# Keys and queries of four batches in two groups of six PSUM banks, in an attention and ELU feed-forward kernel with a planned order

## The chip, the cores and the metric

One core of a Trainium2 chip runs the whole kernel. Times are device microseconds of one execution, from three executions of the kernel before. The core has five engines with a queue each: PE (TensorE, the matmuls), ACT (ScalarE), DVE (VectorE), POOL (GpSimd) and SP (which here only issues transfers). Matmul results go to PSUM, which the code uses as eight banks of 128 x 512 fp32.

## What is computed

The reference is a linear attention with an exponential feature map, and a feed-forward layer with ELU behind it. All tensors are fp32; 8 batches, 8 heads, 576 rows, head size 64, 128 features.

```python
def phi(x):
    proj = np.einsum('bhsd,df->bhsf', x, w_phi)
    proj = proj - np.max(np.abs(proj), axis=-1, keepdims=True)
    return np.concatenate([np.exp(proj), np.exp(-proj)], axis=-1)
q_p, k_p = (phi(q), phi(k))
kv = np.einsum('bhsf,bhsd->bhfd', k_p, v)
z = np.sum(k_p, axis=2)
num = np.einsum('bhsf,bhfd->bhsd', q_p, kv)
den = np.einsum('bhsf,bhf->bhs', q_p, z)[..., None] + 1e-06
...
h = x @ w_in                                   # 4608x512 @ 512x2048
g = np.where(h > 0.0, h, np.exp(np.minimum(h, 0.0)) - 1.0)
out = g @ w_out                                # 4608x2048 @ 2048x512
```

## The kernel before

**Attention by quads.** Four heads of one batch are a quad; there are 16 (`plan_quad`, i = 0 to 15; batch b = i // 2). Of the 576 rows, 512 are the main part and 64 the tail. Keys and queries are transposed (`kT`, `qT`), by PE in the first quads and by SP's transposing transfers from quad 5 on (L555). Then come the projections by `w_phi`. Head size 64 fills only half of PE's rows, so two heads are projected side by side by matmuls of 64 rows (`project_halves`, L672, matmul at L680; `queries_f`, L839, matmul at L843). All other matmuls of the kernel's steady part use 128 rows. The planner calls the 64-row form `mode` 1, and adds 0.095 us to its own estimate for each change of mode.

Per quad the main part makes three kinds of PSUM results. Keys: four banks (`pk`, 16 matmuls), each read by a maximum on DVE (`m_k`, L701) and two exponentials on ACT (`EK`, L739). Queries with rows on the partitions: four banks (`pk`, 8 + 8 matmuls), read by a maximum on DVE only (`m_q`). Queries with features on the partitions: four banks (`pq`, 2 + 2 matmuls of 512 columns), read by two exponentials on ACT each (`Eq`, L906). In batches 2 to 7 they are issued in three groups of four banks: keys; first half of the queries in both forms; second half in both forms (`both`, L867). Tails have small groups of their own with 128 rows.

The rest of a quad: `vs` and `vst` on POOL (L790, L800), `pkv` on PE (L949) with a copy `kv`, `pn` and `pnt` on PE (L1003, L1031), combined by DVE into `tot` (L1052, L1058), divided by DVE and POOL into `x`, transposed into `xT`.

**Feed-forward by chunks.** `plan_chunk` takes 512 rows at a time: eight chunks of main rows, and a ninth made of all tails. A `ph` bank gets four matmuls of 512 columns (L1296, in the first chunk eight of 256, L1311). Then ACT makes `e_sb` (exp, L1324), POOL `u_sb` (minus one, L1328), DVE `gT` (L1340), which frees the bank. A `po` bank takes 16 matmuls over four blocks of 128 rows (L1398), in four ops of four; a copy to `o_sb` on ACT or DVE (L1424) frees it and SP stores it (L1433). The last block of the last chunk is cut into two pieces of 256 columns; their stores are shared between SP and ACT (L1437).

**The order.** Each step is an op with a cost for each engine that can run it, what it depends on, the banks that it takes anew (`new`) and those that it reads (`uses`). `Planner.run` walks through a model of time: for each free engine it takes the ready op with the lowest rank that `fits`. Ranks are a table of two digits per op (`RANKS`, L34). `fits` (L211) caps the banks: a kind `first` or `second` op waits until few enough are held, `ph` has at most four, `po` at most two. Where PE is idle in the model during its first 60 us, it writes filler matmuls (L263 to L268, `fill` L1601). So each engine's instruction order is fixed when the program is built, and at run time each engine follows it and waits for semaphores.

Of the kernel before, what the change touches and what calls it, by code (L numbers as in the profile page):

```python
# [8 lines left out]
FP32 = mybir.dt.float32  # L9
# [25 lines left out]
    "0Q0R0Y0U0l0kHn0+103Y0g0h121B0j14181G161D1I1M1k1F1O1f1L1o1q1r7Q6eBq7B07927YWx4eS7"  # L35
    "04ER1HDHPmPl0KDyDx0LDwD+0HEBDv0JE0E1DzD-251K1p231i1u1v4W5QEWSXEhEpBeEo5I5GS4S2TW"
    "PkPhPj5FS3TUTVPiU9Ud5bUc5SRr97SqU+98SsVQ9IV3V59KSwU-8pV2V4Ti202RUz2C2DVF2f0r8Y8m"
    "H3A8Aw0200064l4dS95JUnEnCQWaQGQHWZQ3OLWVQCP-WhQ5QDWiQ4QBQFQE1h2m261t2a1y2s5P5EUp"
    "UmTgTTTfTZ5O5TUsUrEzSaULUS5RUkUTE+UQUOEd0tGi3IR90x809G0s9g9y1dKwKL0PHuGY7nKKKx7s"
    "2t2u8w3n3VJy3o382q2JDn4KHP2K2G3H1a1m2y3l6k0O934u6M6O2Z9N4T617-2x9V3U8a4R398X2e63"  # L40
    "422p8j2i7A5Y5wEx6R9e3O4hEuAC3c1W01F03W3a2E0EHZ3X3g1T17F24X9F6515Eb485D6f0FBP4q4i"
    "Cx0i9x3R7pCjA3847y5i899bBH3mJ47Z7+223T8+8r3S6V8-418dAA7bDE8V1g7X8JA+BQ4L4f3uSb4+"
    "Pg0m7e3Z8K2v8oDiB7B8DhBSBGDgB3AvHvBRB4VTE-EfBJBI36293534283B33271e9Y9Z787790911l"
    "248O8P2+322-312HEt1V1Z1Y3M8M406J3NHNAq3eHKHt3dHwAr3fA4HQ5C9J9+Ee7P7O5fDo6AAh5HS8"
    "5KUo0n7t3E6N038l8W544z8k5M5N8z5L5cEv5Z5eDeB6BM1X1b3+0o1J0p0q0G0C2F3bEqEr5u5v5t5z"
    "2I1jElEm6u6t6r6q3jEaBXBW7W79D24rDm7a8q8U6wA78u6T8h8s6BAa8y6S8iF37f0W0X6C5aB-AeDI"
    "1c2n7oD1AQ2lIdBh0d2rKqBm7d3xIL4s6s4t9kIGA94MIsA6AF7TFs9lAB3QC39r2w8v3KQp7VEsFQ7q"
    "2MHUF-7lC+7rFp7m7h7UF67JC564CY7c2jBaAV6HC78tAT9s8f9v8nBd2hAUAi5-D71zFK75E2AdAbCM"
    "FH5o5p8FO46p87212B2O2A3P6Y372N3kAs2WCJ4JHO2L4pC69QBDBv9P9OBuBBBCBw9L9MF52Q2PA-B0"
    "9o8C858A8B191A2d8Z8b6P5x5y6K2c9D9E6i6g6h6j5VAM9u9t5s4n4c4m4jBnIVI+50JbIx59IeI-Bi"  # L50
    "JCJ01N6QDZ9h3h3i3r7x5d535+5l2g3JAo4C44An4D45Ap4E4IAm4746867R7S4A499T1C1E3y2o9d9R"
    "3LAfAcAOANARAP3zCRC43v3G3w3F4a4P4H4G3D4VJY9m5B7kFGFn7jF7G17iFZF+9zBO9w7MF8Fo8N7K"
    "7LGQFI8E6l7EG2FrGw7gGJ5rEyBZGPGhBTB5GvGTC11sD5GZAJMSHVETNU4g5kLAMFHBJlBj4oFh3qCI"
    "5AByQqAj3-CEUqAlBzGkP1CXBL96VSCUDRCdRwCZJHCaRvCsL7JURkCuDJIz6WOU9CRRR3RJ6IJi99Fu"
    "IOGf8LSpFT8T8g7GOSLfNG2X2S2U2T9X9aA26Z6-1n43C0BU130y9i0w0zBV0-0vBc0u11IH7u7v1+1-"
    "7262668D6774735WFvFx1R1Q1P1S5mHkHlGjGnGmGlAW9pADAEFN5X76ASGtG6GMGOG8GuHCGXFlGNGW"
    "HDGKEcFqGL5hEYEXDB8I1U2z6D7w5U8SAL514xAK5658AH4y4wAI4-52Cc3t3s574v888382817D8G6L"
    "5n4Y4b2V2Y4k305gDODN6d6c6b6a60Bg1w1x4ZGg4FDu8cCSVwRy9fSdSEAkQuVWCTUlVRCWVvRxRlHg"
    "HhA09A7NLF4UMo8RMd5jLO7FJn3pNHIaNj5qNpIbMuD0DkIDMwFeBpJTDdWeC9CvLjBEJzDUFyBFIXJK"
    "Jx8eSuIuK4HIFcHfHMDcRhJAMDMINEGqFwOpIUGrDCF9MGEwI8KpK3J1ItLQSeM8PRS6D4RWWJBNJEHq"  # L60
    "P0P3DDWgHGCoENWOWYWuLpB26n9n6mGeDr2b2kCKDG68CnOIGzH7ONG+IBOPH8H1OOGyIFJ2CrCtH0G-"
    "550A0D090B0f4Q6GPoPnKcLHKSKR6EOdOeLKLbLaLL9jIq3C3AMcJ3B16FMrEHBrBsClCNC8HxNqBbIh"
    "OgCADsBtBxJ-71700T0SFJFL4BEj69BKJhGHG5KNGCG7KMGFGGJjMBGEUiC26oGDGB4O0b0a4N0Z0c0e"
    "6XNRNQGUGaGVGb6UK7K6MZMVN5MYD6SBE4E5Mv6+NFJcDAHaSvI5GpTqRzRTO7J6RVNTMeRUOaMgRQOm"
    "OlJGJZFP9SWIQIDtAuJVTBKZAgEFHLPeBfKPMzPDDlI3PaOvLRLlQtP7I9CzLMORUgDWLIQVVaKmRSPG"
    "LrKyO9OzVyNSS0PNTaWqSMPLOcVxJdMsO+FAFDOrMiF4IIL5NrFbHTNDRNOwCwScPtDfG0EUESJ8IrEO"
    "L1M9KsU7K5MAMEM-NVGIMK080M8x0NIw0V9qA5FOFS9cCmIWJvJrJWK8K9EiK1K2EgJuJw8QDbDaKAMk"
    "LVKgKeKfKdKjKi9-MHMJLwL-LuLvAtOZOYLSLCLDLTCC7zLgLhLUHpP4HoP5DMIcHJD3QoSADFQJSFCp"
    "WlWsDKSGWvMxCyC-PbQS9BA19HPxAyBoH6KEW9H9WCKIGxKJKFH2KHKGJ5LzL+W8WWFdFiFjFgFkH-Fm"
    "CHQgQdCPCOAzAxCGWwSHTH9W9UTJCkWtTFTGBlQWNcCqRaLeIKHSL8HWFMPJSJL4PFThLGL6JSFEJkVO"  # L70
    "VPQ-IEEkU5OhKDN0LNOCFRMqE7PcFUNPECPpAXNME8QZISRID8P9ImRGDqJMSyRLWFJJS+RHTEJNSzVN"
    "S1InRgNiNfJ7IvKU8HI4RjKYOoEZTnOxNWJLKkNhLiWfL9KhDSI6W1NeKXLYK-I7MtMOMRN7MPUyJsLZ"
    "N2NAT9RdLPObNtTCT7RfOi7C95CL94KbQ9K005OnHHCDHmVlW6W4VjW3W7WRSQSRVnW5SUWUWBWXWGWH"
    "H+KnNJKoWMF1FBOJR4R6TuTrTvTmOQOEO8WnWkWoWpPELJVbUfTYGcP2GdQ7FfG4ICKrJ+KCDYBkHdEP"
    "GRIACeAGIYCBPZQYVzWAPBJDNnKQCfOGJePITcGSPHTbHrU2U3U8U0U6HRO1O0SPSOOjPrOBOAODO6O5"
    "CgI0I1LyM0LxM1CVLoLqPWPVPTPUJtLtQ2Q1M2LkE3NNFVREIgHARMTpQaMTITIiRFRDSxGsIfIlRiHj"
    "HzQnIpNOJBLBMWMNCiVGH5MXQAS5HyMMRKLcNZN9V7LdMhT8RPWSG3N3RcKvSWT6QOKtR+N4JXRmT0T2"
    "MyVmSVT3PYNCGAT5ReKOUhPzO3PMIoTAO-WEO2T1JIPqIyS-POTeNvPyTdTOUJJfQlTsSDUHSCRbP8Ty"
    "UCRpUDQ0VfSkSmUKVEM+NI4SBAWLB9VHWQJ9HFQUQRCFEQHYN+NyHeNmN-HcNsNwHbNuNzJaPwPvU4U1"
    "SgJPJFJOJQHsHiIjFYFXEDEEEAE9JoAYAZEKEMDQDPNLFWEJEIELMmQfMlQxL2M7M5LXLsHELWW0M4ML"  # L80
    "IQM3MjKlM6HXKuTNKaJRP6BYRtUVKWFaFzUbUaIP6x7HQM7I6zQN6v6yTwD9B+UYUXL0MbTRMaDjMpMn"
    "MQFCFFV6UvV8UwKVINIMOtK+OuKzNBQTQeQhRqN8UAN1UBT4SYUeN6TQSZOTNYSSOVSTTLStTKTDG9Tk"
    "TlQmOkTtPsShVgRoLnSLUNSiSIPCR0RnPPUtOHUIToJqNoSlLmQjMCSnROUWQXRsQvUuRYTzPuT-PKUG"
    "LEPQQKSjVoIJQ8T+WDL3QyTxNdTPOfRuVkVAQwUENgQbVZVCSrKTWrTMTjVDSoP+OFVIVKV1V+NbTSVq"
    "WcVdWmMURXQsPfQzR2PXPAUFVhJpTXVBQQWyKBVJRCOqR7V0IkNaUPVMUxOySNVLNXOKWjVcQiTIPSVX"
    "WKNkSKV-JgVYR5VrQrQkQcWdR8VVNlWNRBMfVuVpOXIRW2WbOWNxWTVtPdQ+VUVeWPRAR-CbFtGoH4NK"
    "URChDpE6EVOsR1DLDTDVDXOMV9UMUUViRZUZUjVsSf0IQPEGIZJmQ6QLI2"
# [37 lines left out]
class Planner:  # L125
# [43 lines left out]
    def run(self):  # L169
# [8 lines left out]
        mode = 0  # L178
        pending = []
        landed = []  # L180
        dma = 0.0
# [54 lines left out]
        while todo:  # L236
            started = False
            for e in ready:
                if free[e] > now:
                    continue  # L240
                best = None
                for at, o in ready[e]:
                    if at > now or o.engine or not fits(o, e):
                        continue

                    if any(
                        c < o.cost[e]
                        and free[x] <= now
                        and not any(a <= now and y is not o for a, y in ready[x])
                        for x, c in o.cost.items()  # L250
                    ):
                        continue
                    if best is None or o.rank < best.rank:
                        best = o
# [64 lines left out]
def kernel(  # L319
# [30 lines left out]

    DMA_QUAD = 5
# [161 lines left out]
    def plan_quad(i):  # L513
# [198 lines left out]
        for cs in ((0,), (1,), (2,)) if i == 0 else ((0, 1), (2,)):  # L712
            tail = cs == (2,)

            def keys(e, cs=cs):
                for c in cs:
                    project_halves(0, range(4 * c, 4 * c + 4), main_banks[c])

            o = add(
                {"PE": 0.11 if tail else 0.22 * len(cs)},  # L720
                (lambda e: project(0, 4, tail_bank))
                if tail
                else keys,
                [moved[0][-1] if tail else moved[0][cs[0]], *old("kv"), landed["w_phi"]],
                new=[tail_bank] if tail else [x for c in cs for x in main_banks[c]],
                mode=0 if tail else 1,
                key=first + 0.4 * tail if i != 1 else 0.35 + 0.01 * tail,
            )
            ops["k"].append(o)
            for c in cs:  # L730
                k_of[c] = o
# [96 lines left out]
        ops["q"], m_q, Eq_ops = [], [], {}  # L828
        m_qs = {0: [], 1: [], 2: []}
        for c in range(3):  # L830
# [3 lines left out]
            blocks = slice(c, 8, 2) if halves else slice(4 * c, 4 * c + 4)  # L834

# [29 lines left out]
            if c < 2 and b > 1:  # L865
# [15 lines left out]
            ops["q"] += [o] if o is o_f else [o, o_f]  # L881
# [12 lines left out]
            for par, bank in enumerate(pair_f):  # L894
# [12 lines left out]

                for sg in range(2):
                    Eq_ops[c].append(
                        add(  # L910
                            {"ACT": 0.48 if c < 2 else 0.27},
                            lambda e, sg=sg, f=exp_q: f(e, sg),
                            [o_f, landed["zero"]] if c == 2 else [o_f],
# [3 lines left out]
                    )  # L917

# [357 lines left out]
    def plan_chunk(ch):  # L1276
# [108 lines left out]
        if ch == B:  # L1385
            pieces[-1:] = [(3, 0, DM // 2), (3, DM // 2, DM)]
        for tt, o0, o1 in pieces:
# [3 lines left out]
            for part in range(n_parts):  # L1391
                jts = range(part * N_JT // n_parts, (part + 1) * N_JT // n_parts)

                def mm2(e, tt=tt, part=part, jts=jts, o0=o0, o1=o1, bank=bank):
# [22 lines left out]
                    key=2 * ch + 4.6 + 1.5 * (4 * tt + part) / N_JT + 0.1 * (o0 > 0),  # L1417
                )
                mm2s[ch].append(o)
            t = {}  # L1420

            def out_copy(e, o0=o0, o1=o1, bank=bank, t=t):
                t["o"] = moesm.tile([P, DM], FP32, name="o_sb", bufs=2)[:, o0:o1]
                (nc.scalar.copy if e == "ACT" else nc.vector.tensor_copy)(  # L1424
                    t["o"], bank.tile
                )

            def store(e, tt=tt, o0=o0, o1=o1, t=t):
# [6 lines left out]
                for j, eng in enumerate((nc.sync, nc.scalar)):  # L1435
# [3 lines left out]
                        in_=t["o"][j * TAIL:(j + 1) * TAIL, :],  # L1439
# [6 lines left out]
                [o, back(outs, 2)],  # L1446
# [194 lines left out]
```

## Time and profile before

| | us |
|---|---|
| median of three executions | 359.37 (359.02 to 361.77) |
| the profiled execution | 360.69 |
| its span, first to last instruction | 358.9 |

| engine | busy us | share of the span | instructions |
|---|---|---|---|
| PE | 349.1 | 97% | 3453 |
| DVE | 266.4 | 74% | 575 |
| ACT | 259.2 | 72% | 570 |
| POOL | 242.9 | 68% | 342 |

Busy PE counts a matmul from its start to the modelled end of its way through the array, so matmuls overlap in it; how fast PE works is read from start to start. Whoever an engine waited for is inferred from semaphores. The mean granted clock of PE is 0.995 of full speed.

### The profile page before, as it was taken

How to read it: one execution, taken by the hardware profiler on the slowest of the kernel's cores; microseconds unless marked ns; L12 is line 12 of the kernel's file. 1: busy time of each engine (PE TensorE's matmuls, PEld its weight loads, DVE VectorE, ACT ScalarE, POOL GpSimd, SP SyncE). 2: the span in 40 equal slices, each digit the busy share in tenths (PEclk: the TensorE clock that was granted, in tenths of full speed). 3: DMA queues.
4: the chain of work that ended last, by engine and by line, in shares of the span. 5: the costliest groups of instructions: out<-in, count | busy, mean ns of one | idle time of the engine just before them, and what ended most of it. 6: DMA issues, size and time to landing. Idle time of an engine off the chain costs nothing.

```text
span 358.9 us, 9072 instructions
## 1 busy us (share of the span) xinstructions
PE 349.1 (97%) x3453; PEld 205.5 (57%) x3453; DVE 266.4 (74%) x575; ACT 259.2 (72%) x570; POOL 242.9 (68%) x342
## 2 busy tenths in 40 slices
PE   7898999999999999999999999999999999999995
PEld 6676778656554655455555555555646454444444
DVE  6999699989996889679988989979876466024400
ACT  5997899897778886987889877996594555234411
POOL 9899869699769777867866694299674755034400
PEclk9998999999999999999999999999999999999999
DMA  8999999996886839979966752362130200110013
GB/s 171 232 242 205 211 187 238 142 170 170 147 109 127 123 79 206 173 116 191 151 99 155 154 83 64 92 186 45 35 92 32 62 3 29 58 61 29 29 60 88
DMA packets 84108, 43.46 MB, mean 121 GB/s; under 512 B 54624, under 2 KB 77536, under 8 KB 84064
## 3 DMA queue, kind: packets, MB, share of 16 engines
q1 hardware_dynamic: 57552, 26.59, 33.1%
q0 software_dynamic: 25760, 15.47, 31.1%
q10 hardware_dynamic: 752, 0.82, 0.8%
q8 instruction: 27, 0.44, 0.5%
q14 instruction: 17, 0.14, 0.1%
HBM read 36.77 MB, written 9.44 MB: 129 GB/s over the span
## 4 chain that ended last, share of the span: by engine, by line
PE 91%; ACT 7%; DMA 1%; issue 0%; POOL 0%; SPq 0%; ACTq 0%
PE po L1398 35%; PE ph L1296 31%; PE pkv L949 5%; PE pk L680 5%; PE ph L1311 4%; PE pn L1003 4%; ACT EK L739 3%; PE pq L843 2%; ACT Eq L906 2%; DMA v_b<-in_k_dram 1%; PE pnt L1031 1%; PE tr L619 1%; PE pk L662 1%; ACT EKt L739 1%; PE pq L855 0%; PE pn L1017 0%
## 5 line engine op out<-in xcount | busy, mean ns | idle before, releaser
L1398 PE MATMUL po<-w_out_sb,gT 128*128 128x512 bf16 (+1 forms) x592 | 136.2, 374 | 0.0
L1328 POOL TENSOR_SCALAR u_sb<-e_sb 128x512 bf16<-128x512 f32 x144 | 88.1, 618 | 60.8 <-ACT e_sb L1324 56.3
L1340 DVE SCALAR_TENSOR_TENSOR gT<-u_sb,ph 128x512 bf16<-128x512 bf16 x144 | 95.8, 680 | 40.2 <-POOL u_sb L1328 40.0
L1324 ACT ACTIVATE e_sb<-ph 128x512 f32<-128x512 f32 x144 | 86.5, 610 | 47.8 <-PE ph L1296 43.3
L1296 PE MATMUL ph<-xT,w_in 128*128 128x512 bf16 x448 | 108.4, 380 | 0.0
L1398 PEld LDWEIGHTS <-gT 128*128 128x128 bf16 x592 | 54.7, 98 | 57.9 <-issue 2.4
L906 ACT ACTIVATE Eq<-pq 128x512 bf16<-128x512 f32 x128 | 70.2, 643 | 12.1 <-PE pq L843 11.8
L1296 PEld LDWEIGHTS <-w_in 128*128 128x128 bf16 x512 | 53.6, 114 | 43.1 <-issue 2.1
L739 ACT ACTIVATE EK<-pk 128x512 bf16<-128x512 f32 x128 | 68.1, 641 | 4.3 <-PE pk L680 4.3
L790 POOL TENSOR_TENSOR vs<-v_b,em 128x512 bf16<-128x512 f32 x64 | 65.8, 1048 | 0.0
L701 DVE TENSOR_REDUCE m_q<-pk 128x4 f32<-128x512 f32 (+1 forms) x80 | 47.8, 629 | 11.4 <-PE pk L680 11.1
L701 DVE TENSOR_REDUCE m_k<-pk 128x4 f32<-128x512 f32 (+1 forms) x80 | 47.5, 629 | 7.0 <-PE pk L680 5.2
L1100 POOL TENSOR_TENSOR x<-tot,rec 128x576 bf16<-128x576 f32 x28 | 31.9, 1152 | 13.1 <-DVE rec L1096 13.1
L1424 ACT COPY o_sb<-po 128x512 f32<-128x512 f32 (+1 forms) x26 | 15.0, 577 | 24.8 <-PE po L1398 24.8
L1052 DVE TENSOR_TENSOR tot<-pn,w 128x260 f32<-128x260 f32 x64 | 26.8, 423 | 3.2 <-PE pn L1003 2.0
L1058 DVE TENSOR_TENSOR tot<-tot,pn 128x260 f32<-128x260 f32 x64 | 26.2, 418 | 0.4
L1003 PEld LDWEIGHTS <-Eq 128*128 128x128 bf16 x448 | 19.9, 97 | 8.3 <-issue 0.5
L1003 PE MATMUL pn<-kv,Eq 128*128 128x65 bf16 x448 | 22.4, 194 | 0.0
L949 PEld LDWEIGHTS <-EK 128*128 128x128 bf16 x512 | 18.8, 98 | 3.7 <-issue 0.3
L949 PE MATMUL pkv<-vs,EK 128*128 128x65 bf16 x512 | 20.7, 194 | 0.0
L800 POOL TENSOR_TENSOR vst<-v_tail,em 128x260 bf16<-128x260 f32 x32 | 19.6, 621 | 0.7 <-ACT em L768 0.6
L1311 PE MATMUL ph<-xT,w_in 128*128 128x256 bf16 x128 | 18.2, 280 | 0.0
(92 smaller groups left out, 319.1 us busy)
## 6 DMA issues: line engine op xcount, KB each, us to landing
out_dram<-o_sb SPq DMA_DIRECT2D x32, 256.0 KB, 2.4
v_b<-in_v_dram SPq DMA_DIRECT2D x6, 1024.0 KB, 6.0
k_b<-in_k_dram POOLq DMA_DIRECT2D x7, 512.0 KB, 8.9
q_b<-in_q_dram POOLq DMA_DIRECT2D x7, 512.0 KB, 10.1
w_in<-in_moe_w_in_dram POOLq DMA_DIRECT2D x2, 1024.0 KB, 19.1
w_out_sb<-in_moe_w_out_dram POOLq DMA_DIRECT2D x4, 512.0 KB, 22.0
v_b<-in_v_dram POOLq DMA_DIRECT2D x2, 512.0 KB, 10.0
v_b<-in_v_dram POOLq DMA_DIRECT2D x1, 1024.0 KB, 12.5
```

Of the source, the lines that this page charges most:

```text
L701: nc.vector.tensor_reduce(dst, src, axis=AX.X, op=ALU.max, apply_absolute_value=True)
L739: nc.scalar.activation(EK()[:, 2 * c + par, sg, :] if c < 2 else EKt[:, sg, :], bank.tile[:, 0:n, :].rearrange("p a b -> p (a b)"), ACT.Ex ...
L790: nc.gpsimd.tensor_tensor(st["vs"][:, sg, :, r, 0:D], kqv[b, 2][:, o:o + 2 * HW].rearrange("p (c n d) -> p c n d", c=2, d=D), by_head(st[" ...
L906: nc.scalar.activation(dst, src, ACT.Exp, scale=1.0 - 2.0 * sg)
L949: nc.tensor.matmul(pkv[:, c, sg, :], st["EK"][:, 2 * s + t % 2, sg, (2 * c + t // 2) * F:(2 * c + t // 2 + 1) * F,] if t < NT else EKt[:, ...
L1003: nc.tensor.matmul(pt[:, t, :], st["Eq"][:, par, s, sg, o:o + P], st["kv"][:, s, c, sg, :], start=True, stop=True,)
L1296: nc.tensor.matmul(ph, w_in_of(ct, jt), xTs[ch][:, ct, :] if ch < B else xT_tail[:, ct // 2, :, ct % 2, :], start=(ct == 0), stop=(ct == N ...
L1311: nc.tensor.matmul(bank.tile[:, j, :], w_in_of(ct, jt + j), xTs[ch][:, ct, hf * CHUNK // 2:(hf + 1) * CHUNK // 2], start=(j == 0 and ct == 0),
L1324: nc.scalar.activation(t["e"], flat(bank.tile), ACT.Exp)
L1328: nc.gpsimd.tensor_scalar(t["u"], t["e"], -1.0, 1.0, op0=ALU.add, op1=ALU.mult)
L1340: nc.vector.scalar_tensor_tensor(dst, u, 0.0, bank.tile, op0=ALU.min, op1=ALU.max)
L1398: nc.tensor.matmul(bank.tile, gTs[ch][:, jt, tt * P:(tt + 1) * P], w_out_sb[:, jt, o0:o1], start=(jt == 0), stop=(jt == N_JT - 1),)
```

## The change

There are three edits, and a new table of ranks.

In batches 4 to 7 (`b > MERGED`) the 64-row work of a quad is issued in two groups of six banks: the four key banks with the first two query banks (`q_first`), and the rest, that is the first half's `pq` pair, the second half's `pk` pair and `pq` pair. The exponentials of the first half then hang on the second group. The key group now also depends on the first part of `qT` and on the `pn` ops of the quad two before (`old("out")`).

In the planner, while an op that takes more than four banks is ready and doesn't fit, no op of a later rank that takes a bank may start on that engine.

In the last chunk, the last block is cut into 256, 128 and 128 columns, and the pieces share one `o_sb` tile.

The ranks are new for all ops (2109 before, 2103 after), so the order of every engine differs from the first microseconds on, also in batches 0 to 3. Filler matmuls become 132 where there were 117.

```diff
 RANKS = (
-    "0Q0R0Y0U0l0kHn0+103Y0g0h121B0j14181G161D1I1M1k1F1O1f1L1o1q1r7Q6eBq7B07927YWx4eS7"
+    "0t12141E1R1T8c1U1b6-1H1M1Q1Y1O1f1V1X1Z1k1m1q1u1g1v1r1i1x221tNx4iOS4-074Q7UBL0587"
...
                 best = None
+                first = min(
+                    [o.rank for at, o in ready[e]
+                     if at <= now and len(o.new) > 4 and not fits(o, e)],
+                    default=DONE,
+                )
                 for at, o in ready[e]:
                     if at > now or o.engine or not fits(o, e):
                         continue
+                    if o.new and o.rank > first:
+                        continue
...
-            def keys(e, cs=cs):
+            with_q = b > MERGED and not tail
+            if with_q:
+                q_first = [Bank("first") for _ in range(2)]
+
+            def keys(e, cs=cs, with_q=with_q):
                 for c in cs:
                     project_halves(0, range(4 * c, 4 * c + 4), main_banks[c])
+                if with_q:
+                    project_halves(1, range(4), q_first)
...
-                [moved[0][-1] if tail else moved[0][cs[0]], *old("kv"), landed["w_phi"]],
-                new=[tail_bank] if tail else [x for c in cs for x in main_banks[c]],
+                [moved[0][-1] if tail else moved[0][cs[0]], *old("kv"), landed["w_phi"]]
+                + ([moved[1][0], *old("out")] if with_q else []),
+                new=new + (q_first if with_q else []),
...
-            if c < 2 and b > 1:
+            if c < 2 and b > MERGED:
+                if c == 0:
+                    o, o_f = ops["k"][0], None
+                    ops["q"].append(o)
+                    rest = [(queries_f, pair_f)]
+                else:
+                    rest = [(queries, pair), *rest, (queries_f, pair_f)]
+
+                    def others(e, rest=rest):
+                        for f, _ in rest:
+                            f(e)
+
+                    o = o_f = add(
+                        {"PE": 0.66}, others, deps,
+                        new=[x for _, p in rest for x in p], mode=1, key=key,
+                    )
+            elif c < 2 and b > 1:
...
         if ch == B:
-            pieces[-1:] = [(3, 0, DM // 2), (3, DM // 2, DM)]
+            pieces[-1:] = [
+                (3, 0, DM // 2), (3, DM // 2, 3 * DM // 4), (3, 3 * DM // 4, DM)
+            ]
...
-                t["o"] = moesm.tile([P, DM], FP32, name="o_sb", bufs=2)[:, o0:o1]
+                if o0 == 0:
+                    t["o"] = moesm.tile([P, DM], FP32, name="o_sb", bufs=2)
                 (nc.scalar.copy if e == "ACT" else nc.vector.tensor_copy)(
-                    t["o"], bank.tile
+                    t["o"][:, o0:o1], bank.tile
                 )
```

## Prediction

> **What bounds the kernel now.** I read first, on the page, the shares of the chain of work that ended last and the slice rows of TensorE (PE) and of its clock.
>
> ```profile
> PE   7898999999999999999999999999999999999995
> ...
> PEclk9998999999999999999999999999999999999999
> ...
> PE 91%; ACT 7%; DMA 1%; issue 0%; POOL 0%; SPq 0%; ACTq 0%
> ```
>
> PE carries 91% of the chain. A slice is 9 us: only in the first four (to 36 us) and the last is PE less than full. The list of waits, asked for PE from 60 us to the end, is empty. So after 60 us time leaves only if PE gets less work, and comes only if PE starts to wait. Three stages matter.
>
> The opening, in windows of 2 us (us, then busy time of PE, weight loads, DVE, ACT, POOL, then clock, DMA share, GB/s):
>
> ```profile
> 28.00:30.00 2.00, 1.18 (x34) 1.01 (x30) 2.00 (x6) 2.00 (x5) 1.98 (x3) 1.00 1.30 191
> 30.00:32.00 2.00, 1.16 (x21) 0.80 (x17) 2.00 (x6) 2.00 (x8) 1.99 (x5) 1.00 1.35 205
> 32.00:34.00 2.00, 1.90 (x29) 1.91 (x30) 2.00 (x7) 0.86 (x2) 2.00 (x4) 0.62 1.13 213
> 34.00:36.00 2.00, 2.00 (x17) 1.68 (x15) 1.43 (x6) 1.01 (x1) 1.99 (x4) 0.52 1.16 209
> ```
>
> DVE, ACT and POOL are full while PE has gaps; then PE gets work, and runs it at half clock: in the chain, 16 transposes take 1.71 us there (107 ns each). From 5.7 to about 32 us the chain is mostly ACT (EK and Eq exponentials).
>
> The middle, from the timeline of PE (start, us, line, shape, count):
>
> ```profile
> 200.26 2.76 PE L1296 MATMUL ph<-xT,w_in 128*128 128x512 bf16 x12
> 202.95 0.40 PE L680 MATMUL pk<-w_phi_both,qT 64*128 64x128 bf16 x8
> 203.18 0.38 PE L843 MATMUL pq<-qT,w_phi_both 64*128 64x512 bf16 x2
> 203.49 1.04 PE L1398 MATMUL po<-w_out_sb,gT 128*128 128x512 bf16 x4
> 204.37 1.03 PE L1296 MATMUL ph<-xT,w_in 128*128 128x512 bf16 x4
> ```
>
> Durations include the pipeline's depth, so I read start to start. A 512-column matmul takes 0.216 us (4 po: 203.49 to 204.37, less handing over). Twelve ph end at 200.26 + 2.59 = 202.85; the 64-row query group begins at 202.95: 0.10 us of nothing. Its two 512-column matmuls run side by side on two halves of the rows, end at 203.18 + 0.22 = 203.40, and po starts at 203.49: 0.09 again. Over the later groups the entry gap is 0.092 to 0.106 us, median 0.096.
>
> The end, from the timeline and the DMA issues:
>
> ```profile
> 353.57 0.37 ACT L1424 COPY o_sb<-po 128x256 f32<-128x256 f32 x1 [1.16 <-PE po L1398]
> 355.32 0.37 ACT L1424 COPY o_sb<-po 128x256 f32<-128x256 f32 x1 [1.38 <-PE po L1398]
> 355.72 0.50 ACTq L1437 DMA_DIRECT2D out_dram<-o_sb  x1
> ...
> out_dram<-o_sb ACTq DMA_DIRECT2D x3, 128.0 KB, 2.7
> ...
> out_dram<-o_sb ACTq DMA_DIRECT2D x2, 64.0 KB, 2.2
> ```
>
> After the last matmul: copy 0.37, issue, landing about 2.2, end at 358.9.
>
> [...] 0.096 us a change. [...] clock 0.62 and 0.52 from 32 to 36 us, after 4 us in which PE was busy 58%. [...]
>
> **The change part by part.**
>
> *Grouping.* Per quad of batches 4 to 7 (8 quads) three 64-row groups become two. The changed program's PE order has 47 such groups where the old has 55, so 16 changes of mode fewer: 16 x 0.096 = **-1.54 us**. The 16 + 8 + 8 small and 4 wide matmuls of a quad stay. Inside a group keys and queries follow each other without a gap (at 43.33 us, L843 then L680, 0.22 apart, already so). All these groups lie where PE is full. Bounds: -1.7 (0.106 each) to -1.4.
>
> *Six banks at once.* The group waits until six of eight banks are free; behind it in PE's order stand ph and po, and behind ph the exp of ACT. A ph bank needs, after its matmuls, these three in a row:
>
> ```profile
> L1328 POOL TENSOR_SCALAR u_sb<-e_sb 128x512 bf16<-128x512 f32 x144 | 88.1, 618 | 60.8 <-ACT e_sb L1324 56.3
> L1340 DVE SCALAR_TENSOR_TENSOR gT<-u_sb,ph 128x512 bf16<-128x512 bf16 x144 | 95.8, 680 | 40.2 <-POOL u_sb L1328 40.0
> L1324 ACT ACTIVATE e_sb<-ph 128x512 f32<-128x512 f32 x144 | 86.5, 610 | 47.8 <-PE ph L1296 43.3
> ```
>
> That is 1.91 us, with handing over 2.3 to 2.4 (a ph whose matmuls pass by 289.47 has its gT at 291.74). In the changed order I put beside each of the 16 groups the PE work since the last ops that took a bank. In 14, all but two banks have had the time they need (a kv copy 0.42 plus 0.3, ph 2.4): there po fills the time before. In two they have not: the first has a pn pair 0.96 us back, which needs 1.15 (two tot of 0.42 and 0.3): 0.2 us; the second has ph at 0.1, 0.96 and 2.05 us, of which two may stay: 0.35 us. With queueing unknown I take **+0.4**; bounds 0 (readers run ahead) and 0.35 at all 16, 5.6.
>
> *The key group now also waits for qT.* A transpose of q issued by SP lands 4.0 us later (median); before, one issued at 197.03 was used at 202.95, 1.9 us after landing. I cost it at 0 under that cover; if it goes, PE stops for the lateness, as everything on PE queues behind. Bound 1 us once or twice. SP's queue, where these transposes stand, gets one store more (0.47 us of issue) at the very end; its order moves too, but SP idled 81 us waiting for ACT's o_sb alone.
>
> *New ranks, from the first instruction on.* The work is the same but for four copies that go from DVE to ACT (two of 1024 columns, 1.02 us on ACT; two o_sb of 512, 0.59), under ACT's idle 28% later on. I summed each engine's durations ahead of its first MoE op: ACT 43.1 before and 43.9 after, DVE 39.7 and 38.8, POOL equal. ACT leads the chain there, so up to +0.8; ahead of the 13th op ACT has 0.5 us less to do relative to PE's work. In between: **+0.2**. Bounds: -1.3, if the half-clock window goes (16 transposes at 56 in place of 107 ns are 0.8, twelve 256-column matmuls in 1.3 in place of 1.82 are 0.5), and +1.7, one more such window (half of 3.4). Fifteen more fill matmuls (132 for 117) are 15 x 0.056 = 0.84 us; they stand in gaps of PE and cost 0; with the gaps gone, +0.84. On POOL's queue one w_out load (0.58 us of issue, 512 KB, 2.5 us at the 205 GB/s of that stage) moves ahead of the first w_in, which was issued at 10.3, took 16.8 to 21.5 us to land, and is needed at 34.8: 3 to 7.7 us of cover, so 0, and at worst 0.1 late.
>
> *Last piece.* 16 matmuls of 256 columns (0.109 each, 1.74) become 32 of 128 (0.056, 1.79): +0.05. Copies: 0.58 at 512 and 0.37 at 256 columns, so about 0.27 at 128: -0.10. Landing: 2.7 at 128 KB, 2.2 at 64 KB, so about 2.0 at 32 KB: -0.2. ACT must copy and issue (0.27 + 0.50) within the 0.90 between pieces: it fits. The three pieces share one o_sb, so the last waits for no older store. Sum **-0.25**; bounds -0.4 and +0.1 (if landing has no part that shrinks).
>
> Sum: -1.54 + 0.4 + 0.2 - 0.25 = **-1.2 us**. The profiled execution took 360.69 us (span 358.9 and 1.8 around it); it would take 359.5. It stands 1.3 above the median, so the median goes from 359.37 to **358.2**.
>
> **Rivals.** (1) *Bank holds, slower.* Each six-bank group stops PE until the sixth bank is drained, because ACT, DVE and POOL (72, 74, 68% busy) are late, not just slow. For: before, four banks could stay busy, now two; ACT's queue holds eight exponentials after such a group. Against: PE never waited after 60 us, and po stands ahead of 14 groups. Sixteen holds cancel the gain at 0.10 us each, and pass 1% (+3.6) at 0.33; at 0.35 the time is -1.6 + 5.6: 363.4. (2) *The opening keeps its clock.* For: ten of the new fills stand just before the first ph, where PE was 58% busy. Against: fills cover only half of a gap. -1.54 + 0.4 - 1.3 - 0.25 = -2.7: 356.7. (3) *Given back in the opening*: ACT's +0.8 with part of a clock window or a late load, 1.7 in all. For: the new order foresees more gaps there (15 more fills). Against: engine sums differ by 0.9 at most, in both directions. -1.54 + 0.4 + 1.7 - 0.25 = +0.3: 359.7, no change. (4) *It doesn't do what it says*: excluded, since the groups are counted in the changed order.
>
> **How the numbers follow.** Forecast (357.4 to 359.0): 0.48. Rival 2: 0.20. Rival 3: 0.22. Rival 1: 0.10, most of it past 1%. The range 356.0 to 360.4 takes in the forecast, and most of 2 and 3. One per cent, about what a measurement tells from no change, is 3.6 us: faster than 355.8 needs rival 2 with more, 0.08; slower than 363.0 is most of rival 1, 0.07; within, 0.85.
>
> **What would show it.** Right: 47 groups of 64 rows, entry gaps of 0.096; no PE wait after 60 us beyond half a us in all; last copy 128 columns of about 0.27. Wrong: PE waits at L680's line for ACT or DVE (rival 1) or for a transpose of q; a clock of 1.0 throughout (rival 2); PE continuous only later than about 39 us (rival 3).

## The result, and the profile after

| | before | changed |
|---|---|---|
| median of 20 executions each, us | 359.85 (358.93 to 362.19) | 358.39 (357.98 to 360.07) |
| ratio, 95% interval | | 0.9953 (0.9938 to 0.9968), or -1.7 us |
| profiled execution, us | 360.69 | 358.15 |
| its span, us | 358.9 | 356.4 |
| its mean granted clock | 0.995 | 0.999 |

The forecast of 358.2 held, and so did its sum of -1.2 us, nearly. Its terms did not. I begin with the page of the changed kernel: the slice rows of TensorE (PE) and of its clock, and the shares of the chain that ended last.

```profile
PE   7899999999999999999999999999999999999995
...
PEclk9999999999999999999999999999999999999999
...
PE 85%; ACT 6%; DVE 3%; DMA 3%; issue 2%; POOL 1%; ACTq 0%; POOLq 0%
```

The 8 in the clock row, in the fourth slice, is gone. And DVE, which had no entry in the chain of the kernel before, has 3%: by the list of the chain 4.3 us of it in the opening, 4.7 us at 251 to 256 us, where PE doesn't lose time, and 0.7 us at 136 us, where it does. First the opening of the changed kernel in windows of 2 us (columns as in the prediction):

```profile
28.00:30.00 2.00, 1.72 (x44) 1.46 (x41) 1.97 (x6) 2.00 (x6) 2.00 (x4) 1.00 1.42 198
30.00:32.00 2.00, 1.80 (x32) 1.38 (x31) 2.00 (x6) 2.00 (x8) 2.00 (x5) 1.00 1.27 212
32.00:34.00 2.00, 1.91 (x33) 1.71 (x32) 2.00 (x8) 1.45 (x4) 2.00 (x3) 1.00 1.11 211
```

PE is busy 88% from 28 to 32 us where it was 58%, and no half clock follows. Next, what PE waits for from 60 us on (us in all, times, longest). This list was empty before:

```profile
PE ph L1339 <- DVE gT L1383: 0.5, 1, 0.5
PE po L1443 <- issue: 0.2, 1, 0.2
```

The first of these waits, in PE's timeline (`x16` stands for 16 matmuls; line numbers are those of the changed kernel):

```profile
132.40 1.89 PE L1339 MATMUL ph<-xT,w_in 128*128 128x512 bf16 x7
134.22 0.62 PE L689 MATMUL pk<-w_phi_both,kT 64*128 64x128 bf16 x16
134.70 0.40 PE L689 MATMUL pk<-w_phi_both,qT 64*128 64x128 bf16 x8
135.64 2.98 PE L1339 MATMUL ph<-xT,w_in 128*128 128x512 bf16 x12 [0.55 <-DVE gT L1383]
```

This is the first key group of six banks: 16 key and 8 query matmuls without a gap, 0.48 us from the first key to the first query matmul. It begins on time. Eight `ph` matmuls (one record of them is missing in the trace) end at 132.40 + 8 x 0.216 = 134.13, and the group enters 0.09 us later, the price of the change of mode. PE could have gone on at 134.70 + 8 x 0.028 + 0.096 = 135.02, but the next `ph` starts at 135.64. So PE stops 0.62 us *behind* the group. In the chain of waits the second `ph` behind it starts only at 136.74, where 135.64 + 4 x 0.216 = 136.50 was possible: another 0.24 us, again behind a `gT`.

To compare whole kernels I use one number more, **PE's lag**: the time at which a 64-row group starts, less the summed start-to-start durations of all PE work ahead of it, with 0.096 for each change of mode (also those that a fill causes) and nothing for the fills themselves. It grows only where PE is idle or slow.

| | lag near 65 us | near 134 us | near 143 us | near 265 us | summed work |
|---|---|---|---|---|---|
| before | 21.0 | 21.4 | 21.5 | 22.0 | 333.2 |
| changed | 19.1 | 19.6 | 20.6 | 20.8 | 331.7 |

Four terms can be read off for this pair of executions: work -1.5, opening -1.9, the stretch from 134 to 143 us +0.9 (0.98 against 0.1), the rest about -0.2. Together they make -2.7; the last matmul ends at 352.62 in place of 355.28, 2.7 earlier.

The end of the changed kernel, in ACT's timeline:

```profile
352.70 0.27 ACT L1471 COPY o_sb<-po 128x128 f32<-128x128 f32 x1 [0.62 <-PE po L1443]
353.00 0.50 ACTq L1484 DMA_DIRECT2D out_dram<-o_sb  x1
```

The copy fell from 0.37 to 0.27 us as foreseen. But from the start of the last store to the end of the span it is 3.4 us (353.00 to 356.4), where it was 3.2 (355.72 to 358.9). From the list of transfers of the changed kernel, with the median time to landing at the end:

```profile
out_dram<-o_sb ACTq DMA_DIRECT2D x1, 64.0 KB, 2.2
out_dram<-o_sb ACTq DMA_DIRECT2D x2, 32.0 KB, 2.0
```

The landing did shrink. The last store lands 2.03 us after its start (at 355.03), where it was 2.19 (at 357.91). What grew is the time behind the landing: 1.35 us to the end of the span in place of 0.98. At its end the program has SP wait for one semaphore after the other, 0.06 us apart. By the records of the trace eight of these waits stand behind the last landing (355.04 to 355.50); in the kernel before it was two (357.93 to 358.02). Six waits more are the 0.37 us.

### The profile page after: what moved, and what is told of

It is laid out like the page before. It is cut to its first block, busy times and chain, and to the rows that moved or that the text cites. A ratio compares the mean times of both kernels' runs of the same rounds, so it can differ in the third digit from the quotient of the medians.

```text
span 356.4 us, 9086 instructions
## 1 busy us (share of the span) xinstructions
PE 344.2 (97%) x3439; PEld 205.5 (58%) x3484; DVE 264.4 (74%) x571; ACT 261.6 (73%) x575; POOL 243.5 (68%) x342
## 4 chain that ended last, share of the span: by engine, by line
PE 85%; ACT 6%; DVE 3%; DMA 3%; issue 2%; POOL 1%; ACTq 0%; POOLq 0%
PE po L1443 32%; PE ph L1339 31%; PE pkv L992 5%; PE pk L689 4%; PE ph L1354 4%; PE pn L1046 3%; DMA t_b<-in_q_dram 3%; PE pq L864 2%; ACT Eq L944 2%; ACT EK L757 2%; DVE tot L1095 1%; PE pnt L1074 1%; DVE tot L1101 1%; ACT e_sb L1367 1%; PE pk L671 1%
## 5 line engine op out<-in xcount | busy, mean ns | idle before, releaser
L1443 PE MATMUL po<-w_out_sb,gT 128*128 128x512 bf16 (+2 forms) x584 | 133.0, 368 | 1.3 <-issue 0.2
L1339 PE MATMUL ph<-xT,w_in 128*128 128x512 bf16 x427 | 106.0, 380 | 1.8 <-DVE gT L1383 0.5
L1339 PEld LDWEIGHTS <-w_in 128*128 128x128 bf16 x512 | 54.5, 114 | 45.6 <-issue 3.0
L944 ACT ACTIVATE Eq<-pq 128x512 bf16<-128x512 f32 x128 | 68.7, 638 | 5.6 <-PE pq L864 5.5
L1471 ACT COPY o_sb<-po 128x512 f32<-128x512 f32 (+2 forms) x29 | 16.3, 561 | 30.6 <-PE po L1443 28.7
```

Of the source, the lines that this page charges most:

```text
L944: nc.scalar.activation(dst, src, ACT.Exp, scale=1.0 - 2.0 * sg)
L1339: nc.tensor.matmul(ph, w_in_of(ct, jt), xTs[ch][:, ct, :] if ch < B else xT_tail[:, ct // 2, :, ct % 2, :], start=(ct == 0), stop=(ct == N ...
L1443: nc.tensor.matmul(bank.tile, gTs[ch][:, jt, tt * P:(tt + 1) * P], w_out_sb[:, jt, o0:o1], start=(jt == 0), stop=(jt == N_JT - 1),)
```

## The experiments

All ratios are to the kernel before. "Changed" is 0.9953 in the first job and 0.9940 (0.9919 to 0.9962), 358.34 us, in the job of the runs under "The opening".

### The change undone in part

**ungrouped**: the changed kernel with batches 4 to 7 back in three groups of four banks, the other edits and ranks kept. The planner needs one dependency more, or it blocks itself; added to the changed kernel alone, it leaves PE's order as it is.

```diff
-            with_q = b > MERGED and not tail
+            with_q = b > MERGED and b not in ALONE and not tail
...
-            if c < 2 and b > MERGED:
+            if c < 2 and b > MERGED and b not in ALONE:
...
                 copies + exps + [w] + old("x"),
+                behind=quads.get(i - 1, {}).get("out", []),
```

> The changed kernel with its own opening and its new ranks, but batches 4 to 7 in three groups of four banks again (55 groups of 64 rows, as before; the PE order up to batch 4 is that of the changed kernel, and the third group is put just ahead of the second one's place). A (the prediction): grouping was worth 1.1 us net, the opening nothing, so this kernel takes 1.1 us more than the changed one and about as much as before, less 0.1 to 0.25 for the last piece. B (read from the changed kernel's trace): the opening gave 1.2 to 1.8, and of the 1.5 us of grouping two waits for banks in batch 4 took 1.2 back; so this kernel takes only 0.3 us more than the changed one, and is 1.0 to 1.5 us faster than before. In its trace no jump of PE's lag between 118 and 145 us.

**batch4_alone**: the same for batch 4 only; the first two of its six-bank groups are the two that the prediction named as held.

> The changed kernel with batch 4 alone in three groups of four banks, batches 5 to 7 in groups of six (49 groups). B: the two waits for banks stood at the first two groups, in batch 4; this kernel loses 2 quads x 0.19 = 0.4 us of grouping and saves up to 1.2 us of waits: 0.8 us faster than the changed kernel, with PE's lag flat from 75 us to 260 us. A: 0.4 less than nothing saved, 0 to 0.4 us slower than the changed kernel. If a wait of that size only moves to the first groups of batch 5: 0.4 us slower.

Measured: ungrouped 376.30 us, 1.0455 (1.0419 to 1.0490); batch4_alone 368.89 us, 1.0238 (1.0205 to 1.0271). Every theory missed by 8 us or more. The opening stays good in both (lag about 19.5 near 60 us), and then the lag climbs, to 38 at 276 us in ungrouped and to 30 at 190 us in batch4_alone. The largest waits of PE in the list of ungrouped say why:

```profile
PE ph L1354 <- DVE tot L1109: 1.7, 1, 1.7
PE pk L699 <- DVE gT L1398: 1.5, 1, 1.5
PE pnt L1088 <- DVE tot L1109: 1.3, 1, 1.3
```

With other groups, the same ranks give another order on each engine, and PE waits for DVE again and again. So these two runs don't price the grouping: ranks and groups belong together, and undoing one without the other measures a spoilt order.

**cut_groups**: PE's order as it is, but each of the 16 groups of six banks is cut in two by a matmul of 128 rows and one column. This puts changes of mode back without touching the order. The diff shows the key group; the query group has the same matmul ahead of its first `pq` pair.

```diff
                 if with_q:
-                    project_halves(1, range(4), q_first)
+                    project_halves(1, range(4), q_first, cut=True)
...
+            if cut:
+                nc.tensor.matmul(
+                    pk[0][:, 0, 0:1], zeros, zeros[:, 0:1], start=True, stop=True
+                )
```

> The changed kernel, with each of the 16 six-bank groups cut by one 128-row matmul of one column, whose result is overwritten at once: nothing else moves, but PE changes its mode 32 times more. If a change of mode costs 0.096 us wherever it stands (A and B both): 16 x (2 x 0.096 + 0.03) = 3.6 us more than the changed kernel, +2 us against before. If the changes were hidden, or overlapped with waits for banks: under 1 us more.

Measured: 362.48 us, 1.0064 (1.0042 to 1.0086), 4.0 us above the changed kernel (1.11% of 360.7). Not all of it is changes of mode. The list of PE's waits from 60 us on has one that the changed kernel hasn't, for a transposing transfer at 290 us:

```profile
PE ph L1347 <- DMA xT<-x: 0.8, 1, 0.8
PE ph L1347 <- DVE gT L1391: 0.3, 1, 0.3
```

On the other side the stops around the first key group are shorter: from 118 to 143 us the lag rises 0.85 us in place of 1.25. The 16 added matmuls are 0.2 us by an estimate from the first group in this trace: its one-column matmul starts at 135.01 and the query matmul behind it at 135.12, and these 0.11 us less 0.096 for the change of mode leave some 0.014. So the 32 changes of mode are about 4.0 - 0.8 + 0.4 - 0.2 = 3.4 us, or 0.106 each; the prediction had 0.096, from gaps of 0.092 to 0.106. From 152 to 267 us, where neither kernel stops, the two lags rise alike (0.24 and 0.29), with 26 changes more in cut_groups, each counted at 0.096. The grouping's term stands.

**last_piece**: the kernel before, with the last block cut into 256, 128 and 128 columns, and nothing else.

```diff
-            pieces[-1:] = [(3, 0, DM // 2), (3, DM // 2, DM)]
+            pieces[-1:] = [
+                (3, 0, DM // 2), (3, DM // 2, 3 * DM // 4), (3, 3 * DM // 4, DM)
+            ]
```

> The kernel before with only the last piece cut into 256, 128 and 128 columns; all other instructions in the old order, the opening too. Prediction: -0.25 us. From the changed kernel's trace (3.7 us from the last matmul to the end, where it was 3.6): 0, within 0.2. Its profile is also a second look at the old opening: if the half-clock window belongs to that order, the clock is at half again from about 32 to 36 us; if it came by chance, it is gone or elsewhere.

Measured: 360.78 us, 1.0010 (0.9989 to 1.0031). No gain, though the interval doesn't exclude the 0.25 us forecast (0.9993). Its trace has the end of the changed kernel: copy of 0.27, last store begun at 357.21 and landed at 359.25, eight waits of SP behind it, 3.4 us from its start to the end of the span at 360.6. What copy and landing save comes back behind the landing. Its opening is that of the old order:

```profile
30.00:32.00 2.00, 0.83 (x18) 0.53 (x14) 2.00 (x5) 2.00 (x6) 1.98 (x4) 1.00 1.34 207
32.00:34.00 2.00, 1.41 (x25) 1.18 (x26) 2.00 (x6) 2.00 (x7) 1.99 (x5) 0.98 1.13 212
34.00:36.00 2.00, 2.00 (x30) 2.00 (x27) 1.97 (x8) 0.64 (x2) 2.00 (x3) 0.50 1.16 211
```

Four us with PE busy 56%, and half clock behind it, some 1.5 us later than in the profile of before.

### The opening

**after_again**, **no_fills**, **before_more_fills** and **after_more_fills** ran on one chip. The real work keeps its order on PE in all of them; only filler matmuls differ.

In no_fills (100 fewer):

```diff
-                    if n > 0:
+                    if n > 0 and now < 0.0:
```

In before_more_fills (206 for 117) and after_more_fills (236 for 132):

```diff
-                    n = int(0.5 * (now - max(free[e], banks[filled])) / self.FILL)
+                    n = int(0.95 * (now - max(free[e], banks[filled])) / self.FILL)
```

> The changed kernel once more, on the chip of the three that go with it. Both theories: 0.995 of the kernel before (0.994 to 0.997, as measured), clock 0.999, no window of half clock between 30 and 40 us.

> The changed kernel without the 100 fill matmuls that stand between the end of the opening's 32 and 60 us; the real work is in the same order. Leaves no part of the computation out. Theory A (the fifteen additional fills, or the fills at all, are what keeps PE busy enough that the clock isn't halved): a window of half clock comes back between 26 and 40 us, mean clock about 0.995 or below, and 1.3 to 2 us or more are lost against the changed kernel: ratio 0.999 to 1.003. Theory B (the new order brings PE real work sooner, the fills have no part in it): clock stays at 1.0 there, same time as the changed kernel, 0.995, or 0.3 less because fills can delay real work.

> The kernel before, its order of real work unchanged, with 206 fill matmuls in place of 117 (they fill 0.95 of a foreseen gap, not half). Theory A (busy share of PE ahead of the window decides the clock): the half-clock window at 32 to 36 us goes, mean clock 0.999, and the time falls by 1.3 us (0.8 for transposes and 0.5 for matmuls at full clock): ratio 0.996. Theory B (what the changed kernel gained in its opening is engine work that comes sooner, and the window is only its sign): the clock may recover, but the first L1296 matmul of chunk 1 stays within 0.5 us of 81.4 us: ratio 1.000. A third way: fills stand before real work that was ready and cost up to 89 x 0.056 = 5 us: ratio up to 1.014.

> The changed kernel, its order of real work unchanged, with 236 fill matmuls in place of 132. Theory A and B: the clock is 1.0 there already, so nothing is gained; fills that stand before ready work may cost up to 1 us: ratio 0.995 to 0.998.

| | us | ratio, interval | clock at 0.998 or above |
|---|---|---|---|
| after_again | 358.34 | 0.9940 (0.9919 to 0.9962) | 7 of 7 executions |
| no_fills | 358.49 | 0.9941 (0.9920 to 0.9963) | 3 of 6 |
| before_more_fills | 360.01 | 0.9976 (0.9964 to 0.9989) | 20 of 20 (two more, of 719 and 913 us, left out) |
| after_more_fills | 359.74 | 0.9988 (0.9975 to 1.0001) | 21 of 22 |

Every execution has its own mean clock on record, and that sorts the kernel before by itself. Over the four jobs from ungrouped on, its 120 executions fall into 58 at 0.998 or above, median 359.59 us, and 62 below, median 360.88. **By this sorting the half-clock window costs the kernel before 1.3 us, and comes in about half of its executions.** (The record has only the mean clock of each; where the window lies is known only for those with a trace.) The changed kernel (first job and after_again) shows it in 3 of 27; its other 24 have a median of 358.36. So at equal clock the change is worth 359.59 - 358.36 = 1.2 us, and the rarer window gives the rest. How rare it is varies: swap_only below, with the same opening, has a lower clock in 8 of 22, and there it costs 0.6 us (358.84 against 358.25). The clock isn't all that scatters: of the 24 at full clock, 18 take 357.8 to 358.5 us and six 359.1 to 360.0, and no trace shows why.

In the changed kernel the fills aren't the reason. Without them it takes the same time. In windows of no_fills:

```profile
16.00:18.00 2.00, 2.00 (x28) 1.06 (x24) 2.00 (x5) 1.69 (x9) 2.00 (x4) 0.50 1.23 346
...
20.00:22.00 2.00, 2.00 (x27) 1.44 (x26) 1.59 (x4) 2.00 (x7) 2.00 (x4) 0.66 1.11 207
...
28.00:30.00 2.00, 1.34 (x39) 1.12 (x35) 1.93 (x8) 2.00 (x6) 2.00 (x4) 1.00 1.38 198
30.00:32.00 2.00, 1.51 (x24) 1.08 (x24) 1.99 (x5) 2.00 (x8) 2.00 (x5) 1.00 1.28 210
```

Real work alone keeps PE busy 71% from 28 to 32 us, and the clock stays. Half clock comes earlier instead, from 7.7 to 21.4 us in this trace (mean clock 0.98), and PE is busy six tenths of the first slice of its page, up to 8.9 us. It costs nothing that the time shows: the three executions with it take 358.21 to 358.63, those without 358.19 to 358.54. In the trace the chain is ACT's from 7 to 14.6 us, PE's at half clock up to 22.4, then DVE's and ACT's up to 32.7; the 64-row group that starts at 63.6 and 63.7 us in two traces of the changed kernel starts at 63.9. Theory A for this run falls.

In the kernel before, fills do work on the clock. In windows of before_more_fills:

```profile
28.00:30.00 2.00, 1.85 (x48) 1.45 (x43) 1.97 (x7) 1.77 (x5) 1.78 (x3) 1.00 1.32 196
30.00:32.00 2.00, 1.18 (x20) 0.95 (x20) 2.00 (x5) 2.00 (x7) 1.99 (x4) 1.00 1.35 216
32.00:34.00 2.00, 2.00 (x44) 1.94 (x42) 1.89 (x7) 1.48 (x6) 1.90 (x4) 1.00 1.12 207
```

76% busy over the same 4 us, and the window is gone in all 20 executions, where 62 of 120 without these fills stand below 0.998. But 360.01 is 0.4 above the 359.59 that the kernel before takes at full clock: so much the 89 fills cost. In this trace, at full clock, the lag near 65 us is 0.8 below that of the old order with its window, and 0.8 to 1.0 above that of the new order in its two traces. In after_more_fills, with nothing to cure, 104 fills cost 359.74 - 358.36 = 1.4 us, more than either theory allowed.

### The stop behind the first key group

**short_drain** and **short_elsewhere** leave out the `u_sb` step of POOL for two `ph` tiles; DVE reads `e_sb` in its place, so the minus one is missing in these two tiles of `gT`. PE's order is the same. In short_drain they are steps 11 and 12 of chunk 2, in short_elsewhere steps 2 and 3 of chunk 3.

```diff
-            def minus_one(e, t=t):
+            def minus_one(e, t=t, step=step):
+                if ch == 2 and step in (11, 12):
+                    t["u"] = t["e"]
+                    return
```

> The changed kernel, in which the u_sb step of GpSimd is left out for the two ph tiles that PE computes last before the first key group of six banks (at 134.2 us in the trace of the changed kernel); DVE takes e_sb instead, so those two tiles of gT are max(ph, 0). PE's order is the same. Theory A (PE's stops of 0.62 us at 135.0 and 0.24 us at 136.5 are the drain of exactly these two banks, which hold the only two banks that the group leaves): each drain is shorter by some 0.7 us, both stops go, what PE lags behind its summed work stays within 0.3 us from 122 to 143 us instead of rising by 1.2, and 0.8 us of time are gained: 0.992 of the kernel before, 0.8 below the changed kernel. Theory B (DVE and ACT are late as such, and the lag is only shown there): the stop moves to the next bank or to the next group, and 0 to 0.2 us are gained: 0.994.

> The same step left out for the two ph tiles ahead of another group of six banks, at 151.4 us, where PE doesn't stop (gT is max(ph, 0) for them). Both theories: no time is gained, 0.994, and PE's stop behind the group at 134 us stays at 0.5 us or more. If it gained too, less work for GpSimd as such would be worth something.

Measured: short_drain 357.99 us, 0.9926 (0.9902 to 0.9951), lag from 134 to 143 us +0.63; short_elsewhere 358.34 us, 0.9948 (0.9930 to 0.9967), lag +0.97 as in the changed kernel. The second stop went (the stretch of twelve `ph` takes 2.75 us, not 2.98), the first did not. DVE's timeline of short_drain, and the `ph` behind the group:

```profile
134.28 1.28 DVE L1386 SCALAR_TENSOR_TENSOR gT<-u_sb,ph 128x512 bf16<-128x512 bf16 x2
135.48 0.18 DVE L1138 TENSOR_REDUCE den<-tot 128x18 f32<-128x36 f32 x1
135.69 0.27 DVE L1139 RECIPROCAL rec<-den 128x18 f32<-128x18 f32 x1
135.88 1.22 DVE L1386 SCALAR_TENSOR_TENSOR gT<-e_sb,ph 128x512 bf16<-128x512 f32 x2
...
136.56 2.75 PE L1339 MATMUL ph<-xT,w_in 128*128 128x512 bf16 x12 [0.54 <-DVE gT L1386]
```

DVE has no gap: two older `gT`, then `den` and `rec`, then the `gT` that frees the bank. Its input `e_sb` was ready at 134.45 + 0.60 = 135.05, 0.8 us before. So theory A holds for the second stop and fails for the first, which is DVE's queue.

**swap_short** and **swap_only** move single instructions. The first is short_drain with `den`, `rec` behind that `gT`. The second computes everything, with the same swap on DVE, and on ACT the exponential of that tile ahead of two `Eqt` exponentials. The numbers in the diff, that of swap_only, are ops; swap_short has the first pair alone.

```diff
+BEHIND = {958: 770, 1174: 768, 1175: 768}
...
-                o.fn(e)
+                n = self.ops.index(o)
+                if n in BEHIND:
+                    late.append((BEHIND[n], o))
+                else:
+                    o.fn(e)
+                for x in [x for x in late if x[0] == n]:
+                    x[1].fn(e)
```

> short_drain once more (u_sb left out for the two ph tiles ahead of the group at 134.2 us, gT is max(ph, 0) for them), and on VectorE the pair den, rec stands behind the first of the two gT, not ahead of it; nothing else is moved on any engine. Theory C (what is left of PE's stop in short_drain is VectorE's queue, which has no gap from 131.8 us on: two older gT, den, rec, 0.45 us for the last two, then this gT): the first stop falls from 0.62 us to about 0.2, the second stays away, PE's lag behind its summed work rises by some 0.25 us from 134 to 144 us where the changed kernel has 0.98 and short_drain 0.63. Theory D (the stop has another cause, a bank of the group itself or the exponentials of ACT): it stays at 0.54. In the time 0.3 to 0.4 us below short_drain: ratio 0.991 to 0.992, not to be told apart by the times alone.

> The changed kernel with everything computed; two swaps alone: on VectorE den, rec behind the gT of the first of the two ph tiles, on ACT that tile's exponential ahead of the two Eqt exponentials (0.58 us) that delay it by 0.1 to 0.25 us. Theory C: the gT then waits only for its u_sb, which is ready at 134.75 in place of 134.85, and ends at 135.4 in place of 135.6: the first stop 0.62 becomes 0.35 to 0.5 us, the second stays at 0.24, 0.1 to 0.25 us are gained. Theory D: nothing changes. Ratio 0.993 to 0.994 either way; the trace decides. A third way: rec comes 0.6 us later and something behind it (x on GpSimd) is late, and PE lags more.

Measured: swap_short 357.61 us (six executions), 0.9928 (0.9899 to 0.9957), lag +0.47. DVE's and PE's timeline:

```profile
134.51 0.68 DVE L1394 SCALAR_TENSOR_TENSOR gT<-e_sb,ph 128x512 bf16<-128x512 f32 x1
135.11 0.18 DVE L1146 TENSOR_REDUCE den<-tot 128x18 f32<-128x36 f32 x1
...
135.25 2.83 PE L1347 MATMUL ph<-xT,w_in 128*128 128x512 bf16 x12 [0.20 <-DVE gT L1394]
```

The `gT` starts at once behind its elders, and PE's stop falls from 0.54 to 0.20: theory C. The lag over the stretch goes 0.98, 0.63, 0.47 through the three kernels. The medians, 358.36, 357.99, 357.61, go the same way, but the times don't tell the last two apart: their ratios are 0.9926 and 0.9928. The trace does.

swap_only: 358.39 us, 0.9954 (0.9941 to 0.9968), lag +0.97: nothing gained, and the trace shows the third way at a place I had not named. From ACT's timeline and that of the weight loads:

```profile
134.15 0.66 ACT L952 ACTIVATE Eqt<-pq 128x256 bf16<-128x256 f32 x2
...
134.86 0.22 PEld L697 LDWEIGHTS <-kT 64*128 64x128 bf16 x7 [0.23 <-issue]
```

The stop behind the group is 0.25 us now. But `Eqt`, moved back, ends at 134.81, and the group, in PE's timeline at 134.36, pauses after eight of its 16 key matmuls until 134.86 (the ninth weights are loaded by then). The programs of this kernel and of the changed one give the reason. The group takes the banks 0, 3, 5, 6, 1 and 2, in this order; `Eqt` reads bank 5, the third; and the two `ph` behind the group write into 4 and 7, the two that it leaves. The swap took the stop out behind the group and put it inside. Nothing among these kernels computes the whole result in less time than the changed one.

## Why the prediction was right, point by point

**Grouping, -1.54.** Right in count and size: a change of mode costs PE about 0.1 us, 0.096 by the gaps of the kernel before. Sixteen changes are gone, and cut_groups prices one at 0.106 us by putting 32 back.

**Six banks at once, +0.4.** The mechanism was right, and so were the two groups; the size of one was not. (The two holds foreseen, 0.2 and 0.35, add to 0.55, of which the sum took 0.4.) At the group foreseen to be held 0.2 us, at 122 us, the lag rises by 0.2 up to 134 us, behind the group. In the stretch from 134 to 143 us it rises by about 0.9 more than before, at the group foreseen to be held 0.35 us. The step that failed is "of which two may stay". It asked whether six banks are free at the entry, and they were: the group entered on time. The two banks that may stay were the only ones for the `ph` behind the group, and they drained late: the first needed 2.3 us from its matmuls to the end of its `gT` (133.26 to 135.59), as the prediction had it, and had 1.76 (until 135.02). That is 0.6, and then 0.24 for the second. short_drain and swap_short show whose time it is: the second stop goes with POOL's step, the first needs a place in DVE's queue.

**Key group waiting for `qT`, 0.** Right: the list of PE's waits has no transfer.

**Ranks and opening, +0.2.** Wrong, and the largest error: -1.9 in the pair of profiles, beyond the lower bound of -1.3. The engine sums ahead of the first feed-forward op (ACT +0.8, DVE -0.9) didn't foretell it. About 1.1 of the 1.9 is the window that the profile of before had, 3.41 us at half clock from 32.49 to 35.91 us by its clock records, and that of after had not (360.69 against 359.59 at full clock); the remaining 0.8 comes from the order at full clock. Rival 2 named the window and gave it 0.20, on the ground of the fills, which no_fills excludes. In the traces, near 30 us, half clock came behind 4 us with PE busy 56% (last_piece) and 58% (before), and did not behind 71% (no_fills), 76% (before_more_fills) and 88% (changed). That too little work of PE brings it is an inference from these five; where the limit lies was not shown. Why the same order keeps full clock in half of its executions no trace here shows. What in the new ranks makes the order better by 0.8 was not tried alone.

**Fills, 0.** Right for the fifteen more, since even all hundred are worth nothing here.

**Last piece, -0.25.** About +0.15 in the traces: 3.76 us from the last matmul to the end in place of 3.61. Copy (-0.10) and landing (-0.16) shrank nearly as foreseen. The term that failed is one that the sum didn't have, the time behind the landing, +0.37 by six more waits of SP. And ACT's copy and issue did not quite fit: it is still issuing the store before until 352.66, 0.04 after the last matmul.

**The sum.** -1.2 forecast; -1.2 measured at equal clock, -1.7 over all executions. It is right partly by luck, because errors cancel: 0.5 more stop and 0.4 less gain at the end against 1.0 more gain in the opening at equal clock (-0.8 for +0.2). Of the prediction's own signs, the 47 groups and the copy of 0.27 came; PE's waits after 60 us, 0.7 in the list, are over the half us it allowed, and a clock near 1.0 throughout was the sign of rival 2. Of rival 1, one group in 16 came true; its place, "each six-bank group", was wrong.

## What to carry to other kernels

When a group takes six of eight banks, ask not only whether six are free when it comes, but what the work behind it will write into: the two banks that it leaves, with their readers' queues, set when PE goes on (0.62 and 0.24 us later than it could, here). Where PE has gaps in an opening, sort the executions of one kernel by their clock before comparing kernels: here a window of half clock was worth 1.3 us of 360, as much as the change itself. When a last store is cut smaller, look also at what the program still does after it has landed (here six waits of SP more, 0.37 us). An order that was searched for one grouping can't be used to test another; put a cost back inside the order instead, as cut_groups did.

## What the runs showed of the hardware

A half-clock window costs by its place: 1.3 us at 32 to 36 us, where PE has become the chain, and nothing that the times show at 8 to 21 us in no_fills, ahead of a stretch that DVE and ACT lead. A change between matmuls of 64 and of 128 rows costs about 0.1 us each way: 0.096 by the gaps of the kernel before, 0.106 in cut_groups, which puts a matmul of one column between. A last store of 32 KB landed 2.03 us after its start, one of 64 KB 2.19; and each wait that SP still had to do behind it took 0.06 us, so that six more of them cost more than the smaller store gained.
